# Attention's matmuls gathered into 21 visits, and the late parts normalised two slots earlier

## The chip, the cores and the metric

The kernel runs on one core of one Trainium2 chip. The metric is the device time of one execution in microseconds (us); a small number is better. The times of the kernel before are the median of 3 runs with their lowest and highest. A profile of one more execution records every instruction of the engines: TensorE (PE; PEld is its weight load), VectorE (DVE), ScalarE (ACT), GpSimd (POOL), and SyncE (SP), which only issues DMAs here.

## The reference

Attention without softmax over 8 batches, 8 heads, 576 positions and 64 features per head, its output divided by its root mean square over the 64 features; then two matrix products with a leaky ReLU between them. Cut to what is computed (all float32):

```python
kv = einsum('bhsd,bhse->bhde', k, v)          # q, k, v: (8, 8, 576, 64)
out = einsum('bhsd,bhde->bhse', q, kv)
rms = sqrt(mean(out * out, axis=-1) + 1e-06)
x = (out / rms * g_norm) -> (4608, 512)       # row: batch*576+position, column: head*64+feature
h = x @ w_in                                  # (512, 2048)
return maximum(0.01 * h, h) @ w_out           # (2048, 512)
```

## The kernel before

**Blocks and slots.** The 4608 rows of x are cut into 9 blocks of 512. Block 0 is done by plain products. For blocks 1 to 8 the loop at the end of the kernel (`for i in range(1, NB)`) does both products by Strassen's seven-product scheme, two levels deep from block 2 on, with some quarters three levels deep. A block has 28 slots: 4 chunks `c` of 7 steps `t`, `slot = 7 * c + t`. From block 2 on a slot has one step of the first product (`h_steps`, PSUM banks `ha` and `hb` or `hc` and `hd`) and one of the second product of earlier chunks (`go_o()`, banks `oa` and `oc`); their matmuls use the whole 128 x 128 array. Everything else is put in by slot tables: `go(late, TAIL_SLOTS.get(slot, 0))` advances attention by so many steps. TensorE runs its instructions in the order of the program, and in `steady` blocks (`i` from 2) VectorE's listed instructions do too (`in_turn` and `pin`).

**First product, banks and copies.** A chunk's seven products `k` accumulate into two banks per side; `ORDER = (1, 2, 6, 5, 7, 3, 4)`. Products 1, 2 and 5 begin a bank afresh (`FRESH`), the others add on top. After a product VectorE adds the bank to `qs` (`w_all<-h_..` in the profile) or ScalarE copies it. For the first product of a chunk, t = 0, that copy is put off (`copies`) until VectorE has finished the previous chunk: the generator `h_before` first does that chunk's last additions, `g<-w_all` (a 128 x 1024 add) and `g<-g,w_all`, which read `qs`; then ScalarE applies the leaky ReLU (L864) and runs `copies.pop(0)()` (L1428), which writes `qs` from the banks. The bank that such a copy reads is written again by TensorE two slots on, by product 6, step t = 2.

**Attention.** One batch is 576 rows and a block is 512, so batch b's rows fall on blocks b and b+1, with N of them in the second: 128, 192, 256, 320, 384, 448, 512 for b = 1 to 7. `attention(b)` transposes q (`qT`), forms the product of k and v (`attention_kv`, 36 matmuls for half of the heads, on 64 x 64 tiles of the array; `m` is the half), and then yields from `tails[0]`; `last_tails[b]` keeps `tails[1]`, which the loop runs as `late` in its round i = b. A tail (`tail_of`) is: the product of q with kv (`o_products`, 8 matmuls for each of the two halves e of the features, on 64 x 32 tiles, out to the `att` banks); squares (Square on ScalarE), the scaled copy to x, sums of squares on VectorE; then `divide`: transposes and reductions on VectorE, a square root, `reciprocal`, the spread on ScalarE, and for l = 0 and 1 a transpose `inv` (L421) and a multiplication of x by it (L423). A part with N up to 256 takes both e in one go (`both_outputs`); a wider one takes them at two different slots (`outputs`, e = 0 and 1), because two `att` banks hold one e. From b = 4 on k by v goes into the ends of the `att` banks, behind a q-by-kv product (`kv_beside`) or, in the last step of a narrow part, alone.

**A visit.** A run of attention's matmuls that TensorE does between two of the full-array ones is called a visit here: the array goes to smaller tiles and back. From the first block's late part on the kernel has 30.

**Where the late parts are.** In rounds i = 2 to 7, `TAIL_SLOTS = {1: 1, 4: 1, 5: 2, 6: 1, 8: 2}`: slot 1 runs the first matmul step, slot 4 the second, slot 5 the reductions and the square root, slot 6 the reciprocal and the spread, slot 8 the two `inv` and multiplication steps. In slot 7 VectorE has the previous chunk's additions `g<-w_all` and `g<-g,w_all`. A step put in slot s by this call stands behind the first-product step and the second-product step of that slot in every engine's order.

Of the kernel before, what the change touches and what calls it, by code (L numbers as in the profile page):

```python
# [10 lines left out]
F32 = mybir.dt.float32  # L11
U32 = mybir.dt.uint32
I64 = mybir.dt.int64
AF = mybir.ActivationFunctionType
# [10 lines left out]
def kernel(  # L25
# [36 lines left out]
    nc = tc.nc  # L62
# [33 lines left out]
    def in_turn(ins):  # L96

        if steady or in_line:
            pin(ins)
# [233 lines left out]
    def attention_kv(b, m, kv_ps):  # L333

        two = [(k_ins.pop((b, p)), v_ins.pop((b, p)), p) for p in (2 * m, 2 * m + 1)]
        for j in range(J):
            for i in range(2):
                for k_in, v_in, p in two:
                    r, c = 64 * i, 64 * half_of(p, i)
                    matmul(kv_ps[p % 2][c:c + 64], lhsT=k_in[r:r + 64, j, :],  # L340
                           rhs=v_in[r:r + 64, j, :], start=(j == 0), stop=(j == J - 1))

    def copy_kv(b, kv_ps):
        for i in range(2):
            in_turn(nc.vector.tensor_copy(kvs[b % 2][:, i::2, :], kv_ps[i]))

    def kv_beside(b, m, tiles):

        kv_ps = [t[:, NT - D:] for t in tiles]
        attention_kv(b, m, kv_ps)  # L350
        for i in range(2):
            in_turn(nc.vector.tensor_copy(kvs[b % 2][:, 2 * m + i, :], kv_ps[i]))
        nxt = (b + m, 2 if m == 0 else 0)
        if nxt[0] < B:
            load_kv(*nxt)

    def att_tiles(name):
        return [ps_att.tile([P, NT], F32, tag="att", name=name) for _ in range(2)]

    def kv_tiles():  # L360
        return [ps_att.tile([P, NP // 2, D], F32, tag="att", name="kv_ps") for _ in range(2)]

    def t2k(n, name):
        home = {"tag": name, "bufs": 1} if name[:3] == "sum" else {"tag": "t2k", "bufs": 3}
        return work.tile([P, n], F32, name=name, **home)

    def x_of(lo, hi):
        return block(lo // NT)[:, :, lo % NT:lo % NT + hi - lo]

    def o_products(b, lo, hi, e, o_ps):  # L370
        for p in range(NP):
            for l in range(2):
                r = slice(64 * l, 64 * l + 64)
                matmul(o_ps[half_of(p, l)][E * p:E * p + E, :],
                       lhsT=kvs[b % 2][r, p, E * e:E * e + E],
                       rhs=qTs[b][r, p, lo - b * S:hi - b * S], start=True, stop=True)

    def outputs(b, lo, hi, e, sums, kv=None):


        x, n = x_of(lo, hi), hi - lo
        tiles = att_tiles("o_ps")
        o_ps = [t[:, :n] for t in tiles]
        o_products(b, lo, hi, e, o_ps)
        if kv is not None:
            kv_beside(b + 1, kv, tiles)
        for l in range(2):
            sq = t2k(n, "sq" if e else f"sum{l}")
            nc.scalar.activation(sq, o_ps[l], func=AF.Square)
            if e == 0:  # L390
                sums.append(sq)
            else:
                in_turn(nc.vector.tensor_add(sums[l], sums[l], sq))
        for l in range(2):
            nc.scalar.activation(x[:, 2 * l + e, :], o_ps[l], func=AF.Copy, scale=g_sb[:, e:e + 1])
# [27 lines left out]
            in_turn(nc.vector.tensor_mul(to, to, inv.unsqueeze(1).to_broadcast([P, 2, n])))  # L423
            yield

    def both_outputs(b, lo, hi, sums, kv=None):

        x, n = x_of(lo, hi), hi - lo
        tiles = att_tiles("o_ps")
        o_ps = [t[:, :2 * n].rearrange("p (e n) -> p e n", e=2) for t in tiles]  # L430
        for e in range(2):
            o_products(b, lo, hi, e, [o[:, e, :] for o in o_ps])
        if kv is not None:
            kv_beside(b + 1, kv, tiles)
        squares = []
        for l in range(2):
            sq = t2k(2 * n, "sq").rearrange("p (e n) -> p e n", e=2)
            nc.scalar.activation(sq, o_ps[l], func=AF.Square)
            sums.append(t2k(n, f"sum{l}"))
            squares.append(sq)  # L440

        def add_up():
            for l, sq in enumerate(squares):
                in_turn(nc.vector.tensor_add(sums[l], sq[:, 0, :], sq[:, 1, :]))

        if b != 2:
            add_up()
        for l in range(2):
            for e in range(2):
                nc.scalar.activation(x[:, 2 * l + e, :], o_ps[l][:, e, :], func=AF.Copy,  # L450
                                     scale=g_sb[:, e:e + 1])
        return add_up if b == 2 else lambda: None

    def tail_of(b, lo, hi, fine=False, kv=(None, None)):
        sums = []
        if hi - lo <= N2:
            add_up = both_outputs(b, lo, hi, sums, kv[0])
            yield
            add_up()
            if kv[1] is not None:  # L460
                kv_beside(b + 1, kv[1], att_tiles("kv_ps"))
            yield
        else:
            for e in range(2):
                outputs(b, lo, hi, e, sums, kv[e])
                yield
        for _ in divide(lo, hi, sums):
            if fine:
                yield
        if not fine:  # L470
            yield
# [5 lines left out]
    def attention(b, apart=True, fine=False):  # L477

        qT = qTs[b] = work.tile([P, NP, S], F32, tag="qT", name="qT")
        beside = b > KV_BESIDE  # L480
        kv_ps = None if beside else kv_tiles()

        def turn(p):
            q_in = q_ins.pop((b, p))
            in_turn(nc.vector.transpose(
                qT[:, p, :].rearrange("p (t s) -> p s t", s=T),
                q_in.rearrange("p (s d) -> p s d", d=D)[:, :, :32]))

        def load_q(p):
            n = NP * b + p  # L490
            n += 2 if n <= NP * 3 else 1
            if apart and n < NP * B and n != NP * 3 + 2 or n == NP * 3 + 2 and p == 0:
                to_load.appendleft((n // NP, n % NP, "q"))

        for m in range(2):
            turn(2 * m)
            load_q(2 * m)
            yield
            turn(2 * m + 1)
            load_q(2 * m + 1)  # L500
            if m or b == KV_BESIDE:
                yield
            if kv_ps:
                attention_kv(b, m, [t[:, m, :] for t in kv_ps])
            if not apart and m == 0:
                for p in (2, 3):
                    load_pair(b, p)
            elif apart and not beside:
                load_kv(b + m, 2 - 2 * m)
            yield  # L510
            if apart:
                if m and kv_ps:
                    copy_kv(b, kv_ps)
                yield
        if not apart:
            copy_kv(b, kv_ps)
            yield
        kv = [(None, None), (None, None)]
        if KV_BESIDE <= b < B - 1:
            kv = [(None, 0), (None, 1)] if b == KV_BESIDE else \  # L520
                [(None, 0) if b == KV_BESIDE + 1 else (0, None), (1, None)]
        tails = [tail_of(b, max(i * NT, b * S), min((i + 1) * NT, (b + 1) * S), fine, kv[i - b])
                 for i in (b, b + 1)]
        last_tails[b] = tails[1]
        yield from tails[0]
# [748 lines left out]
    def go(steps, n=None):  # L1274
        while n is None or n > 0:
            if next(steps, steps) is steps:
                return
            n = None if n is None else n - 1
# [91 lines left out]
    for part in range(2):  # L1370
        combine(0, part)

    A_SLOTS = (2, 3, 5, 8, 10, 11, 13, 14, 15, 17)

    TAIL_SLOTS = {1: 1, 4: 1, 5: 2, 6: 1, 8: 2}
    FINE_SLOTS = {16: 1, 17: 2, 18: 2, 19: 9}, {5: 1, 8: 2, 11: 1, 15: 3}
    FINE_3 = {16: 1, 18: 2, 19: 3, 20: 9}, {5: 1, 8: 2, 11: 1, 15: 3}
    FINE_2 = {4: 2, 8: 1, 12: 1, 13: 1, 17: 1, 18: 2, 19: 9}, {2: 1, 3: 1, 12: 1}
    SUM_SLOTS = {22: 2, 23: 1, 24: 1}

    SLOTS_3 = 10, 20, 22, 23
# [21 lines left out]
    for i in range(1, NB):  # L1403
# [6 lines left out]
        for c in range(NC):  # L1410
# [7 lines left out]
            for t in range(7):  # L1418
# [16 lines left out]
                    waited += 1  # L1435
                if not one:

                    go(late, TAIL_SLOTS.get(slot, 0))
                    go(a_steps, fine[0].get(slot, 0))
                    if i + 1 < NB:  # L1440
                        if slot == 22:
                            x_sides, new_quarters, sums, inner = sides_x(i + 1)
                        go(sums, SUM_SLOTS.get(slot, 0))
                        if slot == 25:
                            inner(0)
                        elif slot == 26:
                            inner(1)
                    load_some()
# [99 lines left out]
```

## Time and profile before

| | us |
|---|---|
| median of 3 runs | 909.73 |
| lowest, highest | 909.44, 910.5 |
| the profiled execution, its own time | 909.77 |
| span of its instructions | 908.1 |
| TensorE busy (PE) | 901.6 |
| VectorE busy | 616.1 |
| GpSimd busy | 521.7 |
| ScalarE busy | 330.0 |

The granted clock of TensorE is 1.000 over the span. The span is counted from the first to the last instruction; 1.7 us of the execution lie around it. A line of the profile names the line of the kernel, the engine, the operation, what is written and read (names of the program, buffer numbers left out), the shape, and then busy time and mean duration, or, in the timeline, the start and duration. All additions and subtractions are recorded at line 669 and all matmuls at line 121, so they are told apart by the tensors. A float32 matmul of the program shows as two records, so the 8 of a one-half q-by-kv product are "x16" and the 36 of a half k by v "x72".

### The profile page before, as it was taken

The page shows a single profiled execution, that of the slowest core. Times are in us where ns is not written, and L with a number is a line of the kernel's source. Part 1 is how long each engine was busy: PE and PEld are TensorE (multiplying, and loading weights), DVE is VectorE, ACT ScalarE, POOL GpSimd, SP SyncE. Part 2 cuts the span into 40 slices and gives each one's busy share as a digit, 9 for nine tenths or more (in the row PEclk, how much of TensorE's full clock was granted, in tenths as well). Part 3 has the DMA queues.
Part 4 walks back from the last instruction along what each step waited for, and adds up shares of the span by engine and source line. Part 5 has one row for each costly group of instructions (what it writes and reads, how often), then busy time and mean ns, then how long its engine had stood idle before and what let it go on. Part 6 is the DMA issues. An engine that isn't in the chain of part 4 may idle for free.

```text
span 908.1 us, 19140 instructions
## 1 busy us (share of the span) xinstructions
PE 901.6 (99%) x7344; PEld 788.1 (87%) x7344; DVE 616.1 (68%) x942; ACT 330.0 (36%) x645; POOL 521.7 (57%) x672
## 2 busy tenths in 40 slices
PE   8999999999999999999999999999999999999998
PEld 4555558888998989998999999999999899999997
DVE  5877885676574768685977587666877674646453
ACT  5454523231334332434333343334242424232420
POOL 2000236977638784667647673767477847883730
PEclk9999999999999999999999999999999999999999
DMA  8999918977789679967997698958876768677831
GB/s 253 223 241 234 255 68 264 313 255 243 245 286 335 221 230 300 312 223 250 266 302 275 194 315 274 315 181 255 277 256 190 225 206 277 204 233 224 259 110 59
DMA packets 109530, 219.00 MB, mean 241 GB/s; under 512 B 11776, under 2 KB 51072, under 8 KB 109440
## 3 DMA queue, kind: packets, MB, share of 16 engines
q1 hardware_dynamic: 105504, 212.22, 76.1%
q10 hardware_dynamic: 3488, 4.39, 1.4%
q8 instruction: 58, 0.95, 0.4%
q0 software_dynamic: 448, 1.18, 0.3%
q14 instruction: 32, 0.26, 0.1%
HBM read 187.34 MB, written 30.41 MB: 240 GB/s over the span
## 4 chain that ended last, share of the span: by engine, by line
PE 97%; DMA 1%; DVE 1%; POOL 0%; ACT 0%; issue 0%; ACTq 0%; DVEq 0%; POOLq 0%
PE o_a L121 20%; PE o_c L121 16%; PE h_hc L121 10%; PE h_hd L121 10%; PE h_ha L121 10%; PE h_hb L121 9%; PE o_acc L121 6%; PE h_ps L121 6%; PE o_ps L121 3%; PE h_a L121 2%; PE h_b L121 2%; PE kv_ps L121 1%; PE h_c L121 1%; PE h_d L121 1%; DMA pairs<-in_v_dram 1%; PE o_hc L121 0%
## 5 line engine op out<-in xcount | busy, mean ns | idle before, releaser
L669 POOL TENSOR_TENSOR gs<-g 128x512 f32<-128x512 f32 x62 | 85.5, 1379 | 126.9 <-ACT g L864 65.2
L121 PE MATMUL o_a<-pairs,gs 128*128 128x256 f32 x472 | 111.9, 379 | 0.0
L669 DVE TENSOR_TENSOR o_all<-o_c,o_all 128x256 f32<-128x256 f32 (+2 forms) x124 | 69.5, 560 | 60.3 <-PE o_c L121 46.9
L669 POOL TENSOR_TENSOR w_all<-w_all 128x512 f32<-128x512 f32 x28 | 53.4, 1906 | 88.3 <-ACT w_all L1088 88.2
L864 ACT ACTIVATE g<-g 128x512 f32<-128x512 f32 x124 | 75.7, 630 | 67.8 <-DVE g L669 67.8
L669 DVE TENSOR_TENSOR g<-g,w_all 128x512 f32<-128x512 f32 (+1 forms) x84 | 89.8, 1069 | 11.7 <-POOL w_all L669 5.5
L121 PEld LDWEIGHTS o_a<-pairs,gs 128*128 128x128 f32 x472 | 85.5, 190 | 9.5 <-DVE o_all L669 0.2
L669 DVE TENSOR_TENSOR w_all<-h_ha,w_all 128x512 f32<-128x512 f32 x42 | 28.7, 684 | 55.4 <-PE h_ha L121 53.5
L1088 ACT COPY w_all<-h_hc 128x512 f32<-128x512 f32 x42 | 25.0, 596 | 106.7 <-PE h_hc L121 106.7
L121 PE MATMUL o_c<-pairs,gs 128*128 128x256 f32 x264 | 62.4, 379 | 0.0
L669 POOL TENSOR_TENSOR pairs<-w 128x512 f32<-128x512 f32 x4 | 5.3, 1330 | 98.6 <-DMA stage<-in_moe_w_out_dram 98.6
L669 DVE TENSOR_TENSOR o_all<-o_a,o_all 128x512 f32<-128x512 f32 (+1 forms) x53 | 35.5, 669 | 38.4 <-PE o_a L121 37.8
L669 DVE TENSOR_TENSOR g<-w_all 128x1024 f32<-128x1024 f32 x28 | 35.3, 1260 | 37.1 <-ACT w_all L1088 37.1
L121 PE MATMUL o_a<-w,g 128*128 128x256 f32 x248 | 58.8, 379 | 0.0
L121 PE MATMUL h_ps<-xT,w_all 128*128 128x512 f32 (+1 forms) x136 | 58.1, 571 | 0.3 <-DVE w_all L278 0.3
L121 PE MATMUL o_acc<-w,g 128*128 128x256 f32 (+1 forms) x192 | 57.7, 451 | 0.0
L121 PEld LDWEIGHTS o_acc<-w,g 128*128 128x128 f32 x192 | 36.3, 190 | 21.5 <-issue 17.2
L121 PEld LDWEIGHTS o_c<-pairs,gs 128*128 128x128 f32 x264 | 47.9, 190 | 5.3
L1088 ACT COPY w_all<-h_ha 128x512 f32<-128x512 f32 x42 | 24.8, 592 | 72.8 <-PE h_ha L121 72.8
L121 PEld LDWEIGHTS o_a<-w,g 128*128 128x128 f32 x248 | 45.0, 190 | 4.9
L121 PEld LDWEIGHTS h_ps<-xT,w_all 128*128 128x128 f32 x136 | 25.4, 190 | 26.9 <-issue 24.4
L121 PEld LDWEIGHTS h_ha<-stage,w_all 128*128 128x128 f32 x336 | 42.7, 192 | 3.0 <-issue 1.6
(287 smaller groups left out, 2405.3 us busy)
## 6 DMA issues: line engine op xcount, KB each, us to landing
w_all<-w SPq DMA_DIRECT2D x196, 448.0 KB, 4.7
pairs<-w SPq DMA_DIRECT2D x94, 256.0 KB, 4.5
w<-w SPq DMA_DIRECT2D x22, 448.0 KB, 5.9
v_in<-in_v_dram SPq DMA_DIRECT2D x29, 288.0 KB, 6.2
k_in<-in_k_dram SPq DMA_DIRECT2D x28, 288.0 KB, 6.3
q_in<-in_q_dram SPq DMA_DIRECT2D x46, 144.0 KB, 5.0
q_in<-in_q_dram SPq DMA_DIRECT2D x46, 140.0 KB, 5.4
w<-stage SPq DMA_DIRECT2D x12, 512.0 KB, 4.0
```

The costliest lines, as they stand in the source:

```text
L121: pin(nc.tensor.matmul(*args, **kw))
L669: ins = eng.tensor_tensor(out_, a, b_, op=ALU.subtract if minus else ALU.add)
L864: nc.scalar.activation(t, t if src is None else src, func=AF.Prelu, alpha=SLOPE)
L1088: nc.scalar.copy(q[:, at], bank)
```

## The change

1. *Wide parts in one visit.* A part with N over 256 now may use two more banks: `wide_outputs` forms e = 1 in the banks named by `banks` (`hb` and `hd` in round 1, where they rest; `oa` and `oc` later) and e = 0 in the `att` banks, 32 records at once, and then squares and scaled copies of all four. This is done for batch 2's first part (N = 384), and for the late parts of b = 4 to 7 (N = 320 to 512). The first part of b = 3 (N = 320) still takes two visits.
2. *k by v joined to a q-by-kv visit.* Batch 2's first half of k by v runs behind batch 1's late part (in `hb` and `hd`), batch 3's first half behind batch 2's late part, batch 4's second half behind batch 3's late part and batch 5's first half behind batch 4's first part. Where they are joined they have banks of their own (`flat_bank`). Batch 2's and 3's second halves stay visits of their own (`early`).
3. *Slots.* For all rounds except i = 2 the late part's first matmul step goes to slot 27 of the round before (`go(last_tails[i + 1], 1)`) and the rest is `{2: 1, 3: 2, 4: 1, 6: 2}`: reductions and square root in slot 3, reciprocal and spread in slot 4, both `inv` and multiplication steps in slot 6, where it was 8. Round 2 keeps the old table (`TAIL_2`). `A_SLOTS`, `FINE_2` and `FINE_3` follow the new number of steps.

Each part does the same additions, multiplications and matmuls as before; the order of some instructions and the banks change.

```diff
--- before.py
+++ after.py
@@ -344,12 +344,17 @@
         for i in range(2):
             in_turn(nc.vector.tensor_copy(kvs[b % 2][:, i::2, :], kv_ps[i]))
 
-    def kv_beside(b, m, tiles):
-
-        kv_ps = [t[:, NT - D:] for t in tiles]
-        attention_kv(b, m, kv_ps)
+    def copy_half(b, m, kv_ps):
         for i in range(2):
             in_turn(nc.vector.tensor_copy(kvs[b % 2][:, 2 * m + i, :], kv_ps[i]))
+
+    def ends_of(tiles):
+        return [t[:, NT - D:] for t in tiles]
+
+    def kv_beside(b, m, kv_ps):
+
+        attention_kv(b, m, kv_ps)
+        copy_half(b, m, kv_ps)
         nxt = (b + m, 2 if m == 0 else 0)
         if nxt[0] < B:
             load_kv(*nxt)
@@ -383,7 +388,7 @@
         o_ps = [t[:, :n] for t in tiles]
         o_products(b, lo, hi, e, o_ps)
         if kv is not None:
-            kv_beside(b + 1, kv, tiles)
+            kv_beside(b + 1, kv, ends_of(tiles))
         for l in range(2):
             sq = t2k(n, "sq" if e else f"sum{l}")
             nc.scalar.activation(sq, o_ps[l], func=AF.Square)
@@ -423,7 +428,10 @@
             in_turn(nc.vector.tensor_mul(to, to, inv.unsqueeze(1).to_broadcast([P, 2, n])))
             yield
 
-    def both_outputs(b, lo, hi, sums, kv=None):
+    def flat_bank(tag, name):
+        return ps_m.tile([P, 2, N2], F32, tag=tag, name=name).rearrange("p u n -> p (u n)")
+
+    def both_outputs(b, lo, hi, sums, kv=None, banks=None):
 
         x, n = x_of(lo, hi), hi - lo
         tiles = att_tiles("o_ps")
@@ -431,7 +439,8 @@
         for e in range(2):
             o_products(b, lo, hi, e, [o[:, e, :] for o in o_ps])
         if kv is not None:
-            kv_beside(b + 1, kv, tiles)
+            places = [flat_bank(tag, "kv_ps") for tag in banks] if banks else tiles
+            kv_beside(b + 1, kv, ends_of(places))
         squares = []
         for l in range(2):
             sq = t2k(2 * n, "sq").rearrange("p (e n) -> p e n", e=2)
@@ -451,15 +460,39 @@
                                      scale=g_sb[:, e:e + 1])
         return add_up if b == 2 else lambda: None
 
-    def tail_of(b, lo, hi, fine=False, kv=(None, None)):
+    def wide_outputs(b, lo, hi, sums, kv, banks):
+
+        x, n = x_of(lo, hi), hi - lo
+        apart = [flat_bank(tag, "o_ps") for tag in banks]
+        tiles = att_tiles("o_ps")
+        o_ps = {e: [t[:, :n] for t in ts] for e, ts in ((1, apart), (0, tiles))}
+        for e in (1, 0):
+            o_products(b, lo, hi, e, o_ps[e])
+        if kv is not None:
+            kv_beside(b + 1, kv, ends_of(tiles))
+        squares = []
+        for e in (1, 0):
+            for l in range(2):
+                sq = t2k(n, "sq" if e else f"sum{l}")
+                nc.scalar.activation(sq, o_ps[e][l], func=AF.Square)
+                (squares if e else sums).append(sq)
+                nc.scalar.activation(x[:, 2 * l + e, :], o_ps[e][l], func=AF.Copy,
+                                     scale=g_sb[:, e:e + 1])
+        yield
+        for l in range(2):
+            in_turn(nc.vector.tensor_add(sums[l], sums[l], squares[l]))
+
+    def tail_of(b, lo, hi, fine=False, kv=(None, None), banks=None):
         sums = []
         if hi - lo <= N2:
-            add_up = both_outputs(b, lo, hi, sums, kv[0])
+            add_up = both_outputs(b, lo, hi, sums, kv[0], banks)
             yield
             add_up()
-            if kv[1] is not None:
-                kv_beside(b + 1, kv[1], att_tiles("kv_ps"))
             yield
+        elif banks:
+            yield from wide_outputs(b, lo, hi, sums, kv[0], banks)
+            if fine:
+                yield
         else:
             for e in range(2):
                 outputs(b, lo, hi, e, sums, kv[e])
@@ -477,8 +510,8 @@
     def attention(b, apart=True, fine=False):
 
         qT = qTs[b] = work.tile([P, NP, S], F32, tag="qT", name="qT")
-        beside = b > KV_BESIDE
-        kv_ps = None if beside else kv_tiles()
+        beside, early = b > KV_BESIDE, 1 < b <= KV_BESIDE
+        kv_ps = None if beside or early else kv_tiles()
 
         def turn(p):
             q_in = q_ins.pop((b, p))
@@ -498,8 +531,18 @@
             yield
             turn(2 * m + 1)
             load_q(2 * m + 1)
-            if m or b == KV_BESIDE:
+            if m or early:
                 yield
+            if early:
+                if m == 0:
+                    continue
+                half = [t[:, :D] for t in att_tiles("kv_ps")]
+                attention_kv(b, 1, half)
+                load_kv(b + 1, 0)
+                yield
+                copy_half(b, 1, half)
+                yield
+                continue
             if kv_ps:
                 attention_kv(b, m, [t[:, m, :] for t in kv_ps])
             if not apart and m == 0:
@@ -509,17 +552,19 @@
                 load_kv(b + m, 2 - 2 * m)
             yield
             if apart:
-                if m and kv_ps:
-                    copy_kv(b, kv_ps)
                 yield
         if not apart:
             copy_kv(b, kv_ps)
             yield
         kv = [(None, None), (None, None)]
-        if KV_BESIDE <= b < B - 1:
-            kv = [(None, 0), (None, 1)] if b == KV_BESIDE else \
-                [(None, 0) if b == KV_BESIDE + 1 else (0, None), (1, None)]
-        tails = [tail_of(b, max(i * NT, b * S), min((i + 1) * NT, (b + 1) * S), fine, kv[i - b])
+        if b < KV_BESIDE:
+            kv[1] = (0, None)
+        elif b < B - 1:
+            kv = [(None, 0) if b == KV_BESIDE else (0, None), (1, None)]
+        banks = [{2: ("hb", "hd"), 4: ("oa", "oc")}.get(b),
+                 {1: ("hb", "hd"), 2: None}.get(b, ("oa", "oc"))]
+        tails = [tail_of(b, max(i * NT, b * S), min((i + 1) * NT, (b + 1) * S), fine, kv[i - b],
+                         banks[i - b])
                  for i in (b, b + 1)]
         last_tails[b] = tails[1]
         yield from tails[0]
@@ -1370,12 +1415,13 @@
     for part in range(2):
         combine(0, part)
 
-    A_SLOTS = (2, 3, 5, 8, 10, 11, 13, 14, 15, 17)
-
-    TAIL_SLOTS = {1: 1, 4: 1, 5: 2, 6: 1, 8: 2}
+    A_SLOTS = (2, 3, 8, 10, 11, 13, 15, 17)
+
+    TAIL_SLOTS = {2: 1, 3: 2, 4: 1, 6: 2}
+    TAIL_2 = {1: 1, 4: 1, 5: 2, 6: 1, 8: 2}
     FINE_SLOTS = {16: 1, 17: 2, 18: 2, 19: 9}, {5: 1, 8: 2, 11: 1, 15: 3}
-    FINE_3 = {16: 1, 18: 2, 19: 3, 20: 9}, {5: 1, 8: 2, 11: 1, 15: 3}
-    FINE_2 = {4: 2, 8: 1, 12: 1, 13: 1, 17: 1, 18: 2, 19: 9}, {2: 1, 3: 1, 12: 1}
+    FINE_3 = {13: 1, 18: 2, 19: 3, 20: 9}, {3: 1, 6: 2, 9: 1, 12: 3}
+    FINE_2 = {8: 1, 12: 1, 13: 1, 17: 1, 18: 2, 19: 9}, {2: 1, 3: 1, 12: 1}
     SUM_SLOTS = {22: 2, 23: 1, 24: 1}
 
     SLOTS_3 = 10, 20, 22, 23
@@ -1435,7 +1481,9 @@
                     waited += 1
                 if not one:
 
-                    go(late, TAIL_SLOTS.get(slot, 0))
+                    go(late, (TAIL_2 if i == 2 else TAIL_SLOTS).get(slot, 0))
+                    if slot == 7 * NC - 1 and i + 1 in last_tails:
+                        go(last_tails[i + 1], 1)
                     go(a_steps, fine[0].get(slot, 0))
                     if i + 1 < NB:
                         if slot == 22:
```

## The prediction

> **What bounds the kernel now.** I read the engine table, the chain, TensorE's waits, then the timeline around a visit and around the slots into which the change moves work. From the page, the engines and the chain:
>
> ```profile
> span 908.1 us, 19140 instructions
> PE 901.6 (99%) x7344; PEld 788.1 (87%) x7344; DVE 616.1 (68%) x942; ACT 330.0 (36%) x645; POOL 521.7 (57%) x672
> PE 97%; DMA 1%; DVE 1%; POOL 0%; ACT 0%; issue 0%; ACTq 0%; DVEq 0%; POOLq 0%
> ```
>
> The view of waits, for TensorE:
>
> ```profile
> PE idle_ps L121 <- DVE group L315: 1.5, 1, 1.5
> PE kv_ps L121 <- DMA pairs<-in_v_dram: 0.6, 1, 0.6
> PE sum_ps L604 <- ACT flat L599: 0.4, 1, 0.4
> PE h_ps L121 <- DVE w_all L278: 0.3, 1, 0.3
> ```
>
> TensorE is busy for 99% and is 97% of the chain; its four waits, 2.8 us, lie in the first attention and block 0, which the change leaves alone. So only two things count: TensorE's own time (a visit less is a gain) and new waits of TensorE (now none in the blocks). The margin of the other engines is not seen in those rows; it is the time from the end of a read of a bank to TensorE's next write of it.
>
> A visit, in the timeline of TensorE (start, duration):
>
> ```profile
> 618.61 1.46 PE L121 MATMUL o_c<-pairs,gs 128*128 128x256 f32 x6
> 619.99 0.98 PE L121 MATMUL o_ps<-qT,kv 64*32 64x448 f32 x16
> 620.91 0.49 PE L121 MATMUL h_hc<-xT,w_all 128*128 128x128 f32 x2
> 621.23 0.39 PE L121 MATMUL h_hc<-xt,w_all 128*128 128x128 f32 x2
> ```
>
> 16 records of N = 448 hold TensorE from 619.99 to 620.91. The next two full-array records take 0.32 (620.91 to 621.23) where the pairs after them take 0.22 to 0.23: 0.10 us to come back. Before the visit the last full-array step is 309 ns instead of 216: 0.09 us to go in.
>
> **What the joining saves.** Starts of records give, for a segment of 16, 0.700, 0.806, 0.913, 1.020 us at N = 320, 384, 448, 512: about 0.166 + 0.00167 N. For 32 records, 0.384, 0.598, 0.811, 1.024 at N = 64, 128, 192, 256: 0.171 + 0.00333 N. The fixed part appears once for 32 as for 16, so two visits of 16 made one of 32 save 0.162 of it, plus 0.093 going in and 0.101 coming back: 0.356 us. Five pairs (384 in round 1; 320, 384, 448, 512 late): 1.78 us. Joining k by v (its segment is 1.208 us alone, 1.208 to 1.209 behind a q-by-kv segment) saves the 0.194 of entry and return: four times, 0.78 us. Together **2.56 us**, 21 visits for 30. Matmuls, columns and loads stay the same otherwise. Bounds: none of the 0.162 if four banks break the segment in two (1.75 us), and 2.86 if the visit at 283.38, whose k by v takes 1.507, also lost its 0.30.
>
> The Trainium skill, "TensorEngine Tiling (Array Packing)", section "Key Properties", says that a change of tiling mode, not just of tile, drains TensorE. By that rule a k by v behind a q-by-kv product (64 x 64 after 64 x 32) would pay the drain still, and the four joinings would save nothing: 1.78 in all. The trace disagrees in the rows where both stand together: the q-by-kv segment at 609.53 is 0.913 with k by v behind it and 0.912 without.
>
> **What the new slots cost.** This is the timeline of round 6 (N = 448), slots 7 to 9, VectorE, ScalarE and TensorE:
>
> ```profile
> 627.79 0.69 DVE L669 TENSOR_TENSOR o_all<-o_a,o_all 128x512 f32<-128x512 f32 x1
> 628.40 0.32 DVE L411 RECIPROCAL rms<-rms 128x28 f32<-128x28 f32 x1
> 628.63 1.18 DVE L669 TENSOR_TENSOR g<-w_all 128x1024 f32<-128x1024 f32 x1
> 629.84 2.75 DVE L669 TENSOR_TENSOR g<-g,w_all 128x512 f32<-128x512 f32 x3
> 631.35 0.59 ACT L1428 COPY w_all<-h_hc 128x512 f32<-128x512 f32 x1 [0.88 <-DVE g L669]
> 634.68 1.05 PE L121 MATMUL h_hc<-stage,w_all 128*128 128x128 f32 x8
> 635.57 0.83 PE L121 MATMUL h_hd<-stage,w_all 128*128 128x128 f32 x6
> 635.40 0.62 DVE L421 STREAM_TRANSPOSE inv<-spread 128x448 f32<-128x448 f32 x1
> 636.05 1.92 DVE L423 TENSOR_TENSOR xT<-xT,inv 128x896 f32<-128x896 f32 x1
> ```
>
> At slot 7's begin VectorE adds `o_all<-o_a`, then g; ScalarE copies hc (631.35 to 631.94) and hd (632.68 to 633.27), which wait for those additions; TensorE writes hc again at 634.68, hd at 635.57. Slack: 2.74 and 2.30 us. In the changed program the two `inv` and two multiplications stand right behind `o_all<-o_a`, ahead of `g<-w_all`: queued behind them are g, the leaky ReLU, both copies, and then TensorE's product 6. The reciprocal goes from there (0.23, 628.40 to 628.63). The new wait per round is max(0, B - 0.23 - slack of hd), B being the time of the four.
>
> B, clear of GpSimd: transposes 0.44, 0.50, 0.57, 0.63, 0.70 (mean rows, N = 256 to 512). Multiplications at their shortest: 0.69 (386.45, 512 elements), 0.82 (294.83, 640), 0.94 (193.15, 768); so 0.125 per 128, 1.07 and 1.20 for the two widest (estimates from these). B = 2.25, 2.7, 3.0, 3.4, 3.8. As they run now, beside GpSimd, from the first start to the last end: 349.62 to 353.58 is 3.96; then 3.78, 4.12, 4.65 (635.40 to 640.05), 4.66. Slack of hd: 1.17, 2.11, 2.20, 2.30, 1.33 in rounds 3 to 7; in round 3 VectorE also idles 1.17 before its second g addition, waiting for GpSimd, which takes up as much.
>
> - Clear: 0, 0.36, 0.57, 0.87, 2.24: sum 4.0.
> - Beside GpSimd: 1.4, 1.4, 1.7, 2.1, 3.1: sum 9.7.
>
> Which one? In rounds 4 to 6 GpSimd ends its `w_all<-w_all` 1.1 us into slot 7 (627.46 + 1.27 = 628.73) and then idles 5.67 us; the first multiplication would begin at about 629.1, clear: 1.8 for the three. In rounds 3 and 7 GpSimd is busy to 345.56 and 724.13, right where they would run: between the ends, 0.4 and 2.6. I take **4.8 us**.
>
> Where VectorE does have to take turns is seen in these rows of the same timeline:
>
> ```profile
> 635.75 1.27 POOL L669 TENSOR_TENSOR gs<-gs,g 128x512 f32<-128x512 f32 x1
> 636.98 2.12 POOL L669 TENSOR_TENSOR gs<-g 128x512 f32<-128x512 f32 x1
> 638.56 1.49 DVE L423 TENSOR_TENSOR xT<-xT,inv 128x896 f32<-128x896 f32 x1
> ```
>
> The multiplication at 636.05 takes 1.92 and ends at 637.97, 0.95 after GpSimd's end at 637.02; GpSimd's next then takes 2.12 instead of 1.27. So one stands while the other runs, and whatever of GpSimd's runs beside a multiplication is added to B. The Trainium skill, "SBUF — State Buffer", section "Who interferes with whom", says that a VectorE instruction with two SBUF inputs and a GpSimd one that reads SBUF exclude each other for whole instructions; the trace agrees by that 0.95, and the rule speaks against this change in rounds 3 and 7.
>
> **Other moves.** (a) Four squares and four copies on ScalarE in a row: one e takes 704.88 to 707.12, 2.2 us at N = 512, so all four banks 4.5 at most after the visit; product 1 into `oa` comes one first-product step (1.6 to 2.0) and, where joined, k by v (1.21) after it, with `oa` read first. Round 7 has no k by v: 0 to 0.6, taken 0.1; else 0. (b) Slot 2 of round 2: GpSimd's `stage<-xT` (229.00) now stands behind a gs, two `stage<-xt` and a `pairs<-w,w` that ran after it, 3.6 us; TensorE reads it at 233.90, 2.0 after its end, and has 1.21 of k by v more before it: 0.4, between 0 and 1.3. (c) The k and v loads move with their visits; the nearest is batch 4's second half, now at about 316, with loads issued by 295.2 and landing in 6.3 us (k_in<-in_k_dram row): hidden; uncovered it would cost the rest of 6.3. SP's queue has only such loads and weights. (d) Reductions and roots come some slots sooner: 2 to 3 us of VectorE at slots 3 and 4, off the path while a bank read behind them keeps its 0.3 to 1.4 us; 0, at most 1.
>
> **Sum:** 909.77 - 2.56 + 4.8 + 0.1 + 0.4 = 912.5 in the profiled execution; it stood 0.04 above the median, so about **912.4**.
>
> **Rivals.**
> 1. *Faster: the delayed additions never reach TensorE.* Place: product 6 in slot 9. For it: 2.3 us of slack in rounds 4 to 6, and g's three additions (2.75) could shrink. Against: B is over the slack in four rounds by the shortest rows. It decides at B below slack + 0.23. Then 909.73 - 2.56 = 907.2. Chance 0.19.
> 2. *Even: the shortest sum.* The three waits of rounds 4 to 6 at 1.8, and 0.6 to 1.2 in round 7, since `g<-g,w_all` there takes 3.71 beside GpSimd instead of 2.75 and would run clear later: 2.4 to 3.0, so 909.6 to 910.2, taken 909.9. Chance 0.24.
> 3. *Dearer: the multiplications go beside GpSimd as they do now* (one standing while the other runs, as at 636.05). 909.73 - 2.56 + 9.7 = 916.9, or some 915 if in two more rounds only. It decides where GpSimd's sums reach past slot 7's first 1.1 us. Chance 0.17.
> 4. *The joining does not save*, if the array breaks off between q by kv and k by v or between banks: 0.8 us more than my sum, 913.2. For it no row; against it the 0.913 and 0.912 above. Chance 0.05, inside the forecast's.
>
> **How the numbers follow.** Forecast 0.40 (910.9 to 913.7), and the four chances add to 1. A difference of 0.2%, 1.8 us, is about what a measurement can tell from no change: faster is below 907.9, slower above 911.55. Faster: rival 1, most of it, and a little of 2: 0.20. Same: rival 2 and the low end of the forecast: 0.26. Slower: the rest of the forecast and rival 3: 0.54. The range takes in rival 1's 907.2 and, above, the lower part of rival 3: 907.0 to 915.2.
>
> **What would show it.** In the trace after: 21 visits, the pairs as one segment of 32 of 0.171 + 0.00333 N; in rounds 3 to 7 `inv` right after `o_all<-o_a` in slot 7, the copies of hc and hd 2 to 4 us later against the products, and waits of TensorE at `h_hc<-stage` or `h_hd<-stage` on `ACT w_all L1428`, largest in round 7. If these rows are not there the time is near 907.2 and I am wrong; if the multiplications are 1.4 or longer in rounds 4 to 6, rival 3 has it.

## The result and the profile after

Changed: 917.45 us, median of 9 runs (915.66 to 920.55). Before, on the same chips: 910.5 us, median of 9 (908.92 to 916.13). The ratio is 1.0074, with a 95% interval of 1.005 to 1.0097: 0.74% slower. The profiled execution took 917.63 us, with a span of 915.9 us, 7.8 more than before. In the code of the changed kernel the lines moved: L669 is now L714, L421 and L423 are L426 and L428, L864 is L909, and the postponed copies of L1428 are L1474.

From the page of the changed kernel, the engines and the chain:

```profile
span 915.9 us, 19115 instructions
PE 903.2 (99%) x7344; PEld 792.4 (87%) x7344; DVE 610.8 (67%) x946; ACT 331.0 (36%) x645; POOL 515.6 (56%) x672
PE 88%; DVE 6%; POOL 3%; DMA 1%; issue 1%; ACT 0%; ACTq 0%; DVEq 0%; POOLq 0%
```

The view of TensorE's waits in the changed kernel (who was waited for, us in all, times, longest):

```profile
PE h_hc L121 <- ACT w_all L1474: 4.2, 4, 1.9
PE h_hd L121 <- ACT w_all L1474: 1.5, 4, 1.0
PE h_ha L121 <- POOL stage L714: 0.9, 1, 0.9
```

TensorE's share of busy time still reads 99%. The chain shows the change: TensorE's part of it fell from 97% to 88%, and VectorE (6%) and GpSimd (3%) came in. The three rows of waits are new, and the first two are the forecast ones: product 6 waits for the copies of `hc` and `hd`, which stand behind VectorE's additions of g.

The joined visit of round 6, timeline of TensorE in the changed kernel (start, duration):

```profile
605.64 1.73 PE L121 MATMUL o_ps<-qT,kv 64*32 64x448 f32 x32
607.30 1.28 PE L121 MATMUL o_ps<-v_in,k_in 64*64 64x64 f32 x72
608.51 0.49 PE L121 MATMUL h_ha<-xT,w_all 128*128 128x128 f32 x2
```

Both halves of 448 columns are one segment, 605.64 to 607.30, with k by v behind it: one visit for two. Setting each full-array matmul of one trace against the same one of the other (start after minus start before, in order) prices each edit on TensorE. In round 6 the steps at the old and the new places of the visits add to 2.97 + 0.10 - 2.22 - 0.10 - 1.00 - 0.11 = -0.36 us; rounds 4, 5, 7 and the 384-column part of round 1 give -0.36 each, the four joinings of k by v -0.20 each. **Saved: 2.6 us**, and 0.3 more because the k by v at 283 no longer waited for its load in this execution.

**New waits**, from the same alignment, each with the 0.10 us that the matmul behind it takes longer: 1.22, 1.04, 1.50, 1.85 us in rounds 3 to 6, and 2.19 up to product 6's start in round 7: 7.8 us. Round 7 lost 1.7 more behind that, slot 2 of round 2 has 0.94, product 1 in `oa` in round 7 0.29, and a product in `oa` in round 3 0.18. In all 10.9 of new losses less 2.9 gives 8.0, by which TensorE's last matmuls are later; the spans differ by 7.8.

Round 6 again, changed kernel, timelines of VectorE, GpSimd, ScalarE and TensorE:

```profile
630.12 0.69 DVE L714 TENSOR_TENSOR o_all<-o_a,o_all 128x512 f32<-128x512 f32 x1 [3.56 <-PE o_a L121]
630.73 0.63 DVE L426 STREAM_TRANSPOSE inv<-spread 128x448 f32<-128x448 f32 x1
631.39 1.11 DVE L428 TENSOR_TENSOR xT<-xT,inv 128x896 f32<-128x896 f32 x1
632.43 0.63 DVE L426 STREAM_TRANSPOSE inv<-spread 128x448 f32<-128x448 f32 x1
633.09 1.91 DVE L428 TENSOR_TENSOR xT<-xT,inv 128x896 f32<-128x896 f32 x1
634.92 1.21 DVE L714 TENSOR_TENSOR g<-w_all 128x1024 f32<-128x1024 f32 x1
...
631.51 1.31 POOL L714 TENSOR_TENSOR more<-g,more 128x128 f32<-128x128 f32 x1
632.78 1.27 POOL L714 TENSOR_TENSOR w_all<-w_all 128x512 f32<-128x512 f32 x1
...
637.67 0.59 ACT L1474 COPY w_all<-h_hc 128x512 f32<-128x512 f32 x1 [0.87 <-DVE g L714]
...
638.31 1.16 PE L121 MATMUL h_hc<-stage,w_all 128*128 128x128 f32 x8 [1.14 <-ACT w_all L1474]
639.64 0.60 PE L121 MATMUL h_hd<-stage,w_all 128*128 128x128 f32 x3 [0.17 <-ACT w_all L1474]
```

`g<-w_all` starts 4.2 us after the start of the first `inv` and TensorE writes `hc` at the very end of its copy. The first multiplication took 1.11, the second 1.91: GpSimd's `more<-g,more` and `w_all<-w_all` run beside it, to 634.05. In the kernel before, GpSimd's last of these ended 0.94 after the start of `o_all<-o_a`; here it is 3.9 after.

### The profile page after: what moved, and what is told of

Read it like the earlier page. It is cut to its first block, busy times and chain, and to the rows that moved or that the text cites. A ratio compares the mean times of both kernels' runs of the same rounds, so it can differ in the third digit from the quotient of the medians.

```text
span 915.9 us, 19115 instructions
## 1 busy us (share of the span) xinstructions
PE 903.2 (99%) x7344; PEld 792.4 (87%) x7344; DVE 610.8 (67%) x946; ACT 331.0 (36%) x645; POOL 515.6 (56%) x672
## 3 DMA queue, kind: packets, MB, share of 16 engines
q10 hardware_dynamic: 3488, 4.39, 1.4%
## 4 chain that ended last, share of the span: by engine, by line
PE 88%; DVE 6%; POOL 3%; DMA 1%; issue 1%; ACT 0%; ACTq 0%; DVEq 0%; POOLq 0%
PE o_a L121 18%; PE o_c L121 14%; PE h_hd L121 9%; PE h_ha L121 9%; PE h_hc L121 8%; PE h_hb L121 8%; PE o_acc L121 6%; PE h_ps L121 6%; PE o_ps L121 3%; DVE g L714 2%; PE h_a L121 2%; PE kv_ps L121 1%; DVE xT L428 1%; PE h_c L121 1%; DMA k_in<-in_k_dram 1%
## 5 line engine op out<-in xcount | busy, mean ns | idle before, releaser
L714 POOL TENSOR_TENSOR gs<-g 128x512 f32<-128x512 f32 x62 | 83.3, 1344 | 142.8 <-DVE w_all L714 68.4
L714 DVE TENSOR_TENSOR o_all<-o_c,o_all 128x256 f32<-128x256 f32 (+2 forms) x124 | 69.5, 560 | 65.2 <-PE o_c L121 52.0
L909 ACT ACTIVATE g<-g 128x512 f32<-128x512 f32 x124 | 75.7, 633 | 92.2 <-DVE g L714 92.2
L714 POOL TENSOR_TENSOR w_all<-w_all 128x512 f32<-128x512 f32 x28 | 49.4, 1763 | 86.4 <-ACT w_all L1133 86.3
L714 DVE TENSOR_TENSOR g<-g,w_all 128x512 f32<-128x512 f32 (+1 forms) x84 | 85.2, 1014 | 11.7 <-POOL w_all L714 5.9
L714 DVE TENSOR_TENSOR o_all<-o_a,o_all 128x512 f32<-128x512 f32 (+1 forms) x53 | 35.5, 670 | 60.7 <-PE o_a L121 60.1
L714 POOL TENSOR_TENSOR pairs<-w 128x512 f32<-128x512 f32 x4 | 5.3, 1327 | 98.6 <-ACT cut L262 98.6
L714 DVE TENSOR_TENSOR w_all<-h_ha,w_all 128x512 f32<-128x512 f32 x42 | 28.7, 684 | 39.4 <-PE h_ha L121 36.8
L714 DVE TENSOR_TENSOR g<-w_all 128x1024 f32<-128x1024 f32 x28 | 36.1, 1290 | 27.4 <-ACT w_all L1133 27.4
L121 PE MATMUL h_hc<-stage,w_all 128*128 128x128 f32 x336 | 45.6, 279 | 4.2 <-ACT w_all L1474 4.2
```

Of the source, the lines that this page charges most:

```text
L121: pin(nc.tensor.matmul(*args, **kw))
L714: ins = eng.tensor_tensor(out_, a, b_, op=ALU.subtract if minus else ALU.add)
L909: nc.scalar.activation(t, t if src is None else src, func=AF.Prelu, alpha=SLOPE)
```

## The experiments

**Slot 8 again.** Everything of the change but the place of the last two steps.

```diff
-    TAIL_SLOTS = {2: 1, 3: 2, 4: 1, 6: 2}
+    TAIL_SLOTS = {2: 1, 3: 2, 4: 1, 8: 2}
```

> The changed kernel with one difference: in rounds 3 to 7 the two inv and multiplication steps stand in slot 8 again, as before the change; joined visits, matmuls in slot 27, reductions in slots 3 and 4 stay. Theory (the four VectorE instructions ahead of g in slot 7 make TensorE wait in slot 9): the waits at h_hc and h_hd on the copies of L1474 go, 7.7 us in all with their restarts, and with the longest of them the stretch of half clock behind it, 1.8 us; what stays is the saving of the visits, the 0.94 at slot 2 of round 2 and 0.29 at oa: about 908. Rival (the matmuls' move to slot 27 alone makes GpSimd and VectorE late): waits of 3 us or more stay, at these banks or others, 911 or more.

Measured: 908.15 us (907.79 to 912.0), ratio to before 0.9988 (0.9978 to 0.9998); run again beside another kernel, 908.03 and 0.9985 (0.9974 to 0.9996). The waits of TensorE in that kernel:

```profile
PE idle_ps L121 <- DVE group L315: 1.5, 1, 1.5
PE h_ha L121 <- POOL stage L714: 0.8, 1, 0.8
PE kv_ps L121 <- DMA pairs<-in_v_dram: 0.6, 1, 0.6
PE o_ps L121 <- DMA v_in<-in_v_dram: 0.4, 1, 0.4
```

No row for the copies of L1474 is left; 0.28 us stays at `h_hd` in round 3 by the alignment. The two steps in slot 6 cost the changed kernel all that it lost, and the joined visits are worth their 2.6 less the 0.9 and the 0.3. GpSimd tells more. Its timeline in this kernel, round 6, with VectorE's:

```profile
626.94 0.69 DVE L714 TENSOR_TENSOR o_all<-o_a,o_all 128x512 f32<-128x512 f32 x1 [3.56 <-PE o_a L121]
629.04 1.69 DVE L714 TENSOR_TENSOR g<-g,w_all 128x512 f32<-128x512 f32 x2
631.90 1.22 DVE L714 TENSOR_TENSOR g<-g,w_all 128x1024 f32<-128x1024 f32 x1 [1.17 <-POOL w_all L714]
...
630.14 1.73 POOL L714 TENSOR_TENSOR w_all<-w_all 128x512 f32<-128x512 f32 x1
```

GpSimd's last sum ends at 631.87, 4.9 us after `o_all<-o_a` starts, though no multiplication stands there: the rest of the change by itself makes GpSimd late in slot 7. Here that costs VectorE a wait of 1.17, and TensorE nothing in this round.

**Slot 6 in the kernel before.** Visits as they were, the last steps two slots sooner.

```diff
-    TAIL_SLOTS = {1: 1, 4: 1, 5: 2, 6: 1, 8: 2}
+    TAIL_SLOTS = {1: 1, 4: 1, 5: 3, 6: 2}
```

> The kernel before with one difference: reciprocal and spread in slot 5, the two inv and multiplication steps in slot 6; visits where and as they were. Theory (half of the dearer multiplications comes from GpSimd, which the visits' move made late by 3 us): GpSimd ends about 1 us into slot 7 as before, the multiplications of rounds 4 to 6 run clear of it (0.8 to 1.1 us), waits in rounds 3 to 7 of 4 to 5 us in all, longest 2.2 in round 7: 914 to 915. Rival (the visits' move has no part in it): the multiplications are as long as in the changed kernel and the waits sum to 7.7, and half clock after: 918 to 920.

Measured: 914.54 us (914.36 to 922.2), ratio 1.0073 (1.0047 to 1.01). The time is in my band, and the rival's 918 is out. The profile: 4.7 us of span more than before. The multiplications of round 6 (VectorE's timeline in this kernel), and GpSimd's last sum, which had ended at 629.65:

```profile
630.71 1.09 DVE L423 TENSOR_TENSOR xT<-xT,inv 128x896 f32<-128x896 f32 x1
632.39 1.09 DVE L423 TENSOR_TENSOR xT<-xT,inv 128x896 f32<-128x896 f32 x1
...
628.38 1.27 POOL L669 TENSOR_TENSOR w_all<-w_all 128x512 f32<-128x512 f32 x1
```

Both at 1.09, my clear value. Waits with restarts: 0.7, 0.2, 0.7, 1.7, 2.1 in rounds 3 to 7, 5.4 in all, a little above my 4 to 5. Part of round 6's 1.7 is not the multiplications: the reciprocal, now in the crowded slot 5, waited 0.38 for its square root and pushed `o_all<-o_a` to 629.31, 0.77 after product 1 had begun (0.20 in the changed kernel). So the slots alone, without the visits' move, cost 4.7 us of span, against 7.8 for the whole change, which has the saved visits on the other side; the two ratios differ by less than their intervals.

**Fewer sums on GpSimd.** The changed kernel without the eight small sums of one inner set of g from round 3 on; the products that use that set take old values.

```diff
-                        if 2 <= t:
+                        if 2 <= t and (t < 6 or i < 3):
-                if c % 2 and now - 3 in begun and t == 0 and two_of_3(now - 3):
+                if c % 2 and now - 3 in begun and t == 0 and two_of_3(now - 3) and i < 3:
```

> The changed kernel, leaving out from round 3 on the eight 128x128 additions of GpSimd for one inner set of g (so the products that use them take old values): GpSimd is through 3.4 us sooner. Theory (GpSimd's additions beside the multiplications lengthen them and g's additions): B falls to its clear value (3.4 in round 6, from 4.2), the waits of rounds 3 to 7 fall from 7.7 to 4 to 5 us, the longest to under 2 and half clock with it: 912 to 914. Rival (VectorE's own work alone makes the wait): waits unchanged, 917.

Measured: 914.96 us (912.27 to 918.96), ratio 1.0062 (1.004 to 1.0083); the median lies above the expected band, the lowest run in it. Its profile (914.08, span 912.4, clock 1.000) holds a wait of 1.3 us for v's load at 285 which lies ahead of round 3 and so of the edit. VectorE's round 6, and GpSimd's last sum:

```profile
630.68 1.09 DVE L428 TENSOR_TENSOR xT<-xT,inv 128x896 f32<-128x896 f32 x1
632.36 1.09 DVE L428 TENSOR_TENSOR xT<-xT,inv 128x896 f32<-128x896 f32 x1
...
629.25 1.27 POOL L714 TENSOR_TENSOR w_all<-w_all 128x512 f32<-128x512 f32 x1
```

GpSimd is through at 630.52, 1.1 us after `o_all<-o_a` starts (629.40). Waits with restarts are 1.22, 0.22, 0.62, 1.02, 2.18 us in rounds 3 to 7, 5.3 in all, a little above my 4 to 5: rounds 4 to 6 fell from 4.39 to 1.86. That difference, 2.5 us, is GpSimd's share there; the rest, 1.86, is VectorE's own work. Round 3 did not change, and in round 7 the wait at `hc` fell from 1.92 to 1.48 (the 2.18 holds 0.4 at `hd`, which the changed kernel has inside its stretch at half clock). Half clock was absent from the profile, but 3 of the 6 runs had a mean clock of 0.998 or lower, and no trace shows where.

**Slot 6 in round 7 alone.** Slot 8 in rounds 3 to 6, slot 6 in round 7.

```diff
+    TAIL_7 = {2: 1, 3: 2, 4: 1, 6: 2}
-                    go(late, (TAIL_2 if i == 2 else TAIL_SLOTS).get(slot, 0))
+                    go(late, (TAIL_2 if i == 2 else TAIL_7 if i == 7 else TAIL_SLOTS).get(slot, 0))
```

(with `TAIL_SLOTS` as in the first experiment.)

> The changed kernel with the inv and multiplication steps back in slot 8 in rounds 3 to 6, and in slot 6 in round 7 alone. Theory: one wait of about 2.1 us in round 7, right behind it 3.4 us of granted clock 0.5 that cost 1.8 us: about 3.9 us more than with slot 8 in all rounds, 911 to 912. Rival (half clock comes from the sum of all rounds' waits, or by chance of the run): clock 1.000 and only 2.1 us more, 910.

Measured: 912.63 us (911.18 to 917.81), ratio 1.0035 (1.002 to 1.005), somewhat above my 911 to 912. Against the trace with slot 8 throughout, TensorE is 3.98 us later at the end than at the wait's begin: 2.10 at `h_hc`, 0.34 at `h_hd`, 0.10 for each restart, and the rest at half clock. The table by stretches of 1 us of this kernel (bounds, length, busy TensorE with records, granted clock, DMA share, GB/s):

```profile
727.00:728.00 1.00, 0.00 (x0) 1.00 0.43 167
728.00:729.00 1.00, 0.18 (x1) 1.00 0.66 244
729.00:730.00 1.00, 0.98 (x8) 1.00 0.01 2
730.00:731.00 1.00, 0.85 (x6) 0.81 0.00 0
731.00:732.00 1.00, 1.00 (x6) 0.50 0.00 0
732.00:733.00 1.00, 1.00 (x7) 0.50 0.59 82
733.00:734.00 1.00, 1.00 (x7) 0.50 0.81 319
734.00:735.00 1.00, 1.00 (x10) 0.98 0.15 57
```

TensorE stands for 1.9 us, and 1.8 us after it starts again its clock is 0.50 for about 3.4 us. The mean clock of the run was 0.998 or lower in 8 of the 12 runs, 1.000 in the other four, whose times (911.18, 911.29, 912.51, 913.68) overlap with the rest; of the 23 runs of the kernel before on the same chip, 2 had a mean below 1.000. So one such wait is enough, without the other rounds' waits, and half clock seems to follow it often, not always.

**One pair in slot 6.** The first `inv` and multiplication in slot 6, the second pair in slot 8.

```diff
-    TAIL_SLOTS = {2: 1, 3: 2, 4: 1, 6: 2}
+    TAIL_SLOTS = {2: 1, 3: 2, 4: 1, 6: 1, 8: 1}
```

> The changed kernel with only the first inv and multiplication in slot 6 in rounds 3 to 7, the second pair in slot 8. Theory (a wait comes only from what exceeds the slack of the copies): the delay is half, about 1.6 to 2.1 us in rounds 4 to 6 with a slack of 2.1 to 2.3, so next to no wait there; up to 0.6 in round 3 and up to 1.2 in round 7; clock 1.000: 908.5 to 910. Rival (the wait goes with the delay in proportion): half of 7.7, some 912.

Measured: 911.25 us (910.77 to 914.13), ratio 1.003 (1.0018 to 1.0042). Above my band, nearer the rival's 912, though not by the rival's way: the waits at `h_hc` are gone but for 0.1 in round 6, and what is left stands at `h_hd`, 0.7, 0.3, 0.35, 0.54, 1.03 us in rounds 3 to 7 (2.9 in all, 2.6 more than slot 8). The delay is a pair and, what half of B did not contain, GpSimd's hold on g's additions. VectorE and GpSimd in round 6 of this kernel:

```profile
634.10 3.70 DVE L714 TENSOR_TENSOR g<-g,w_all 128x512 f32<-128x512 f32 x3
...
632.94 2.25 POOL L714 TENSOR_TENSOR w_all<-w_all 128x512 f32<-128x512 f32 x1
```

The three additions take 3.70 where they take 2.75 with both pairs ahead, when GpSimd is through before they start. What is saved at the second multiplication is paid in part here.

**Slot 7.** Both steps in slot 7, behind g and the two copies.

```diff
-    TAIL_SLOTS = {2: 1, 3: 2, 4: 1, 6: 2}
+    TAIL_SLOTS = {2: 1, 3: 2, 4: 1, 7: 2}
```

> The changed kernel with both inv and multiplication steps in slot 7 in rounds 3 to 7: behind the additions of g and the two copies in the program, ahead of the next product's additions. Theory (what matters is to stand ahead of g): no waits on the copies of L1474 but those of slot 8's kernel (0.3 in round 3); VectorE's additions from ha and hb come up to 4 us later, which they may have to within 1 us: 908 to 911. Rival (any place before slot 8 costs the same): 915 or more.

Measured: 914.24 us (913.41 to 918.18), ratio 1.0062 (1.0047 to 1.0077). The waits of TensorE in this kernel:

```profile
PE h_ha L121 <- DVE w_all L714: 4.5, 4, 1.5
```

The copies are free, and the next bank is not: the four instructions now stand ahead of `w_all<-h_ha`, and TensorE's write of `ha` waits 0.76, 1.15, 1.62, 1.62 us in rounds 4 to 7. I had let these additions come 4 us later at 1 us at most. In round 6 the four instructions take 3.8 (634.97 to 638.74 on VectorE) and TensorE waits 1.6: the slack was 2.2. In slot 8 the steps stand behind these additions too.

**GpSimd's order at the end of round 1.** Slot 8, and round 1's table changed so that the scheduler puts `stage<-xT` ahead of the last sums of g again.

```diff
-    A_SLOTS = (2, 3, 8, 10, 11, 13, 15, 17)
+    A_SLOTS = (2, 3, 5, 8, 10, 13, 15, 17)
```

> The changed kernel with the inv and multiplication steps in slot 8 in rounds 3 to 7, and with A_SLOTS (2, 3, 5, 8, 10, 13, 15, 17) in round 1, which leads the scheduler to put GpSimd's stage<-xT ahead of the last two sums of g at the end of round 1, as it stood before the change. Theory (the 0.9 us wait at slot 2 of round 2 comes from that order on GpSimd): the wait on GpSimd's stage goes, 0.9 to 1.0 us less than with slot 8 alone: 907 to 907.3. Rival (the joined k by v or VectorE's order makes it): the wait stays, 908.1.

Measured: 908.85 us (907.19 to 911.21), ratio 0.9994 (0.9985 to 1.0003), span of the profile 905.5 (1.6 below slot 8's 907.1, of which 0.7 is a load of v that came sooner at 285). Run once more beside slot 8 alone:

> The kernel of slot 8 in rounds 3 to 7 once more, beside the one with GpSimd's order changed too, on one chip. Theory: 1.3 us below the kernel before, 908 where that one has 909.3. Rival (the savings of the joined visits are lost in the spread of the loads): within 0.5 of the kernel before.

> The kernel with slot 8 and GpSimd's old order at the end of round 1, beside slot 8 alone on one chip. Theory: the 1.0 us that its trace shows less (0.91 of wait and 0.10 of restart) is there in the times as well, 907.0 to 907.5, lowest run included. Rival (its other change, batch 2's second k by v a slot sooner, meets loads that are late in some runs): lowest run 1.0 us lower, but the median no better than slot 8 alone.

Measured: 908.03 (907.87 to 913.29) for slot 8 alone; 907.85 (907.04 to 912.52) with the order, ratio 0.9988 (0.9973 to 1.0003). In both traces the wait on `POOL stage` is gone, so the 0.94 at slot 2 came from GpSimd's order. Its lowest runs are 0.6 to 0.8 below those of slot 8 alone, the medians +0.7 and -0.2 (the first pair on two chips): in times the gain is not shown. The profiles of the later pair hold other waits: 3.2 us for v's load at 92, in block 0, with slot 8 alone; 0.4 at `o_a` with the order. That batch 2's second k by v, a slot sooner, meets late loads is not shown by them, and why half of the runs lie 1 to 5 us above the lowest stays open.

Slot 8 alone is the one version that the intervals put below the kernel before, by 0.12 and 0.15%.

## Why the prediction failed

The sign and the place of the new waits were right; their size was not, because one overlap of VectorE and GpSimd was ruled out wrongly: 912.4 forecast with 915.2 as upper end, 917.45 measured.

- *What the joining saves*: forecast 2.56, measured 2.6, pair by pair 0.36 (0.356) and 0.20 (0.194). Joined k by v paid no second drain: the two tilings stand together as before. Rival 4 is out.
- *The place of the new wait*: as forecast, product 6 in slot 9, on the copies of `hc` and `hd`, in rounds 3 to 7, largest in round 7. Taking the two steps back to slot 8 removed it. Rival 1 is out.
- **The step that failed** is the choice under "Which one?": "In rounds 4 to 6 GpSimd ends its `w_all<-w_all` 1.1 us into slot 7 (627.46 + 1.27 = 628.73) and then idles 5.67 us; the first multiplication would begin at about 629.1, clear: 1.8 for the three." Measured: 4.39 for the three. I read GpSimd's place in slot 7 from a trace whose slots 1 and 4 held two visits, in round 6 3.4 us of TensorE's time together (2.32 and 1.11), which the same change moves ahead of slot 0. The first and the last sum of GpSimd's chain before, and its first three after:

```profile
610.40 1.27 POOL L669 TENSOR_TENSOR gs<-g 128x512 f32<-128x512 f32 x1 [4.37 <-DVE w_all L669]
627.46 1.27 POOL L669 TENSOR_TENSOR w_all<-w_all 128x512 f32<-128x512 f32 x1
...
614.66 1.27 POOL L714 TENSOR_TENSOR gs<-g 128x512 f32<-128x512 f32 x1 [6.96 <-DVE w_all L714]
616.01 1.74 POOL L714 TENSOR_TENSOR gs<-gs,g 128x512 f32<-128x512 f32 x1
617.71 1.66 POOL L714 TENSOR_TENSOR gs<-g 128x512 f32<-128x512 f32 x1
```

The chain, 18.3 us from 610.40 to 628.73 before, starts at 614.66 and takes 19.4 after, and TensorE goes through these slots in less time. By the slot GpSimd ends 3.0 us later: its start is 1.9 nearer to `o_all<-o_a` (15.5 ahead of it, 17.4 before), and the chain is 1.1 longer. In the chain, two `gs` sums beside `sum<-sum,sq`, which the change moved to slot 3, take 1.74 and 1.66 instead of 1.28. The move of the visits and that of the reductions were not run apart. The cover that I named was gone by the change's own doing. With GpSimd's chain cut short the three rounds gave 1.86, my 1.8.

*What the step is worth.* The profiled execution is 5.1 us above its forecast (917.63, 912.5). Rounds 4 to 6 make 2.6 of it; 1.7 is the stretch behind round 7's wait, 0.4 rounds 3 and 7 (1.22 and 2.19 measured, 0.4 and 2.6 forecast), 0.9 the other moves; 0.5 went the other way (the load at 283, and 0.2 after TensorE's last matmul).

- This is rival 3 by its own condition, "where GpSimd's sums reach past slot 7's first 1.1 us". By its sign, multiplications of 1.4 or longer, rounds 5 and 6 have it (1.84 and 1.91 for the second one) and round 4 nearly (1.36). Its 9.7 was too much (7.8 measured, restarts included, before the rest of round 7): the first multiplication of rounds 5 and 6 ran nearly clear (0.96 and 1.11), and in round 7 both did (1.23 and 1.22). There GpSimd was the one that stood, its `more<-more,g` at 726.63 taking 1.33 instead of 0.46, and g's additions paid later: 3.69, as before the change (3.71). Rival 2 had counted on 2.75 there and on 1.8 for rounds 4 to 6; it is out.
- *The 0.10 us of restart* after each wait was not in my sum, though the profile before shows the same 0.10 at every return to the full array: 0.8 us over eight waits.
- *Half clock in round 7* was in no case of mine: 1.7 us behind the wait of 2.1, with what is left of the wait at `hd`.
- *Other moves*: (b) 0.4 forecast, 0.94 measured, within its 0 to 1.3; (a) 0.1 forecast, 0.29 measured in round 7, within its 0 to 0.6; the 0.18 before `oa` in round 3 was in none of them, and its cause is open; (c) and (d) cost nothing that shows on TensorE.

The Trainium skill's rule on VectorE and GpSimd ("SBUF — State Buffer", section "Who interferes with whom") fits what was measured: a multiplication of round 6 takes 1.09 us alone and 1.91 beside a GpSimd sum. It can only be used with GpSimd's place in the changed program, which I had not worked out.

## What to carry to other kernels

Where a change moves matmuls out of some slots, every engine that keeps its place by slots loses that time: work out the covering engine's place anew before a row of the old trace is used as cover. A step may be put ahead of other work on an in-order engine only by the smallest slack behind it; here one place had 1.2 to 2.3 us, another 2.2, and in round 6 the steps took 3.8 and 4.2. A share of 99% busy says nothing of such waits: the chain and the bank's slack do.

## What the runs showed of the hardware

A wait of TensorE of about 2 us was followed by half clock. In the changed kernel TensorE stood for 1.92 us to 734.04; in its table by stretches of 1 us the granted clock is the third figure from the end:

```profile
733.00:734.00 1.00, 0.00 (x0) 1.00 0.58 184
734.00:735.00 1.00, 0.96 (x7) 0.82 0.21 78
735.00:736.00 1.00, 1.00 (x6) 0.50 0.00 0
736.00:737.00 1.00, 1.00 (x6) 0.50 0.00 0
737.00:738.00 1.00, 1.00 (x7) 0.50 0.00 0
738.00:739.00 1.00, 1.00 (x11) 0.97 0.79 168
```

Half clock begins 0.6 us after the restart and lasts 3.41 us (734.64 to 738.05); full-array steps take 0.21 instead of 0.11. Six of the 9 runs had a mean clock of 0.998, as this one; the other three (1.000, 0.999, 1.000) are the three fastest, 915.66 to 916.1 against 917.12 and more.

The traces show more than the length of the wait. Before the fall the clock had been at 1.00 for 727.04 us here, for 723.63 with slot 6 in round 7 alone, and for 88.75 in the second execution of slot 8 alone, where a wait of 3.25 us for v's load was followed by half clock too: 213, 212 and 26 times 3.413 us. So the falls lie on a grid of steps of 3.41 us. In the step ahead of these three falls TensorE stood for 1.92, 1.79 and 2.59 us in all; the most in a step without a fall behind it is 1.50, in the kernel of one pair in slot 6. A wait that lies across the edge of two steps would then count less in each, which may be why the same wait does not bring half clock in every run; no trace shows that. The Trainium skill, "TensorE: Matmul & The Clock Gate", section "Part 1: The HAM clock gate (the "warmup" mystery)", gives the same two states and a free-running window of 3.4 us, and the 3.4 us at half rate and the grid agree with it; but it lets the clock fall after an idle window of that length, and here 1.8 us of idle time in a step were enough.
